# Smaller rings for two inputs, a larger ring for outputs, and new places for the moved work in a fused attention and highway kernel

## The chip, the cores and the metric

The kernel runs on one core of one Trainium2 chip. A core has five engines with instruction streams of their own: PE (matrix products), DVE and ACT (elementwise work on 128 partitions), POOL (elementwise work, and here the issue of all loads that convert from float32 to float16) and SP (here the issue of nearly all output stores). Sixteen DMA engines move the data. Within one engine's stream the order is fixed when the program is built; engines wait for one another through semaphores.

The metric is the device time of one execution in microseconds (us). Before the change the median of eight runs is 275.14 us (274.88 to 275.33).

## What is computed

Four batches (B = 4) of N = 6336 rows and C = 256 channels. The first half is a cross-covariance attention, whose attention matrix is channels by channels; the second half is a highway layer on its output:

```
qn = q / (norm of q over the N rows + 1e-6);  kn = k / (norm of k over the N rows + 1e-6)
a  = softmax over the last axis of (kn^T qn / tau)      # 256 x 256 for each batch
x  = v a                                                # N x 256 for each batch
H  = relu(x w_h);   T = sigmoid(x w_t + b_t)
out = T H + (1 - T) x
```

Inputs and output are float32. So each batch needs all rows of q and k before its 256 x 256 matrix is known, and only then can its rows of v be turned into output.

## The kernel before, in words

**Two kinds of work, run side by side.** A batch's 6336 rows are 49 tiles of 128 rows and a remainder of 64. *Pass 1* of a batch adds up, over its 49 tiles and the remainder, S = k^T q and the diagonal blocks of k^T k and q^T q (the Gram matrix G) in PSUM: `p1_tile` (L209 on), six matmuls a tile (lines L227, L230, L233). Its tiles come from loads of q and k in groups of mostly eight tiles, `load_q` and `load_k` (L127 to L137). Groups are counted through all batches here: 0 to 6 are batch 0's, 7 to 13 batch 1's, 14 to 20 batch 2's, 21 to 27 batch 3's. For some runs of tiles (`SQ_RUNS`) the q^T q part is not made on PE: ACT squares q (L275), DVE adds up the squares (L300) and PE sums the partitions (L322).

*The slots* make the output. There are 100 slots, 25 a batch; slot t handles a pair of row tiles. In slot t PE transposes the pair of v tiles (L574; DVE copies them back to SBUF as `vts`, L587), then multiplies the transposed pair by three 256 x 256 matrices of the batch (line L601): into `zbank` for the gate, into `h` for the relu branch and into `x`. ACT makes the gate `tt` by a sigmoid of `zbank` (L655) and writes the bias into the bank for the next use, the seed (L659). DVE makes `th` = max(h, 0) tt (L671) and `ux` = (tt - 1) x (L676); POOL subtracts them into an output tile (L686). The `th` and `ux` tags have four buffers each, and `h` and `x` share three PSUM banks.

*The chain* of a batch (`chain`, L308) stands between its pass 1 and its slots: norms from G, reciprocals (`invs`, L375), two diagonal tiles `dcat` on ACT (L377), the broadcast `cq` on PE (L396), the scaled logits (L409), exponentials on ACT (L419), the softmax scaling (L440), transposes of the matrix (L456), and its products with the two weight matrices (`ah`, L466), copied into the three matrices of the slots.

**The order.** Batch 0's pass 1 and chain come first, alone. Then the loop over slots (L882) interleaves: slots of batch b, the tiles of pass 1 of batch b + 1, and the steps of chain b + 1, which are placed by tables that give for each step a slot after the end of pass 1 and a position in it (`EARLY` for batch 1, `MID` for batch 2, `LAST` for batch 3). Pass 1 of batches 1 to 3 ends near slots 18, 42 and 63 (`P1_END`). From slot 64 on only the slots of batches 2 and 3 and the last chain are left.

Some steps can run ahead of their slot. `GATES` gives the number of gates in a slot where it isn't one, `TURNS` the number of pairs transposed; a 2 moves one step ahead, a 0 lets the lead shrink by one. In the slots of `PE_BIAS` the gate's bias is added by two matmuls on PE (L595) instead of by ACT's seed. `TGROUPS` names two groups of six v tiles of batch 3 that the DMA transposes instead of PE, and the slot in which SP issues it.

**Loads.** POOL issues each load in its own stream, among its subtractions. A load waits there for its buffer (`QRING` buffers each for q and k, four for v) and for the load issued eight earlier, since eight semaphores take turns. For batches 1 to 3 a planner at build time decides after which slot a load stands: it keeps a list ordered by due slot (`want`, which uses `RAMP`), holds a load back until its buffer's last reader has been emitted and until, by its own count of transfer time (`START_US`, `SLACK`), few enough are under way (`next_loads`, L737). By the same count it decides how many tiles of pass 1 go into a slot. Batch 0's groups up to `QRING` are issued at the start, ahead of the identity matrix that POOL also makes; the rest after the first tile of group 1.

**Stores.** The output tile of four slots is stored as 1 MB by SP (`send_store`, L635). Stores are held back so that loads go first: `DEFER` groups stay unsent, and each slot in `DRAIN` lowers that number by one for the rest of the run. The ring of output tiles has `ORING` buffers.

The lines that the change sets, and the functions around them:

Of the kernel before, what the change touches and what calls it, by code (L numbers as in the profile page):

```python
# [19 lines left out]
def kernel(  # L20
# [30 lines left out]
    def spans(*sizes):  # L51
        got, s0 = [], 0
        for ns in sizes:
            got.append((s0, ns))
            s0 += ns
        assert s0 == NS
        return got
# [3 lines left out]
    QALL = [(b, g) for b in range(B) for g in range(len(QG[b]))]  # L61
    QFIRST = [QALL.index((b, 0)) for b in range(B)]
    QTILES = 8
    QRING = 6
    ORING = 6
    DEFER = 5
    DRAIN = [57, 78, 74, 84]
    VG = [spans(6, 10, 12, 12, 9)] + [spans(12, 12, 12, 13)] * (B - 1)
    VTILES = 13
    VALL = [(b, g) for b in range(B) for g in range(len(VG[b]))]  # L70
# [1 line left out]
    VRING = 4  # L72
    NPAIR = (NS + 1) // 2
    LOOK = 3
    RAMP = 13
    REM_SLOT = 2
    START_US = 2

    WARM = (14, 9)

# [1 line left out]
    HEAD = sum(CHAIN0)  # L82
    P1_END = [18, 42, 63]

    GATES = {17: 2, 20: 0, 27: 2, 51: 2, 52: 2, 55: 2, 58: 0, 66: 0, 69: 0, 73: 0, 95: 2}
    TURNS = {49: 2, 51: 2, 52: 2, 53: 0, 59: 1, 60: 2, 64: 0, 72: 0, 73: 0, 93: 2}
    VTS = 9
    OLAST = 2
    TTS = 6

    TGROUPS = ((26, 6, 78), (38, 6, 79))

    PE_BIAS = (18, 21, 83, 97)

    DVE_SUBS = (98, 99)

# [2 lines left out]

    SQ_RUNS = {1: (6, 14, 21, 28), 2: (17, 26, 35), 3: (9, 23, 33)}
    SQ_TILES = 8
    SQ_CUTS = 4
    SQ_RATE = 2
    LULL = [2, 3, 0, 5]

    EARLY = {"sums": (0, "pre"), "norms": (0, "pre"), "invs": (1, "pre"), "cq": (1, "pe"), "logits": (2, "pre"), "exps": (2, "post"), "softmax": (4, "pre"), "at": (4, "pe"), "at_copy": (5, "pre"), "ahat": (5, "pe"), "ahat_copy": (6, "pre")}
    MID = {"sums": (0, "pre"), "norms": (0, "pre"), "invs": (2, "pre"), "cq": (2, "pe"), "logits": (2, "post"), "exps": (3, "post"), "softmax": (3, "post"), "at": (5, "pe"), "at_copy": (6, "pre"), "ahat": (6, "pe"), "ahat_copy": (7, "pre")}
    LAST = {"sums": (0, "pre"), "norms": (0, "pre"), "invs": (2, "pre"), "cq": (2, "pe"), "logits": (2, "post"), "exps": (3, "pre"), "softmax": (7, "pre"), "at": (8, "pe"), "at_copy": (9, "pre"), "ahat": (9, "pe"), "ahat_copy": (10, "pre")}  # L110
    PLACES = [None, EARLY, MID, LAST]

    ctx.enter_context(tc.manual_schedule())
# [7 lines left out]
    def rows(src2d):  # L121
        return src2d[0:NF, :].rearrange("(p s) c -> p s c", s=NS)
# [4 lines left out]
    def load_q(n):  # L127
        b, g = QALL[n]
        s0, ns = QG[b][g]
        q_t[n] = stream_pool.tile([P, QTILES, C], f16, tag="q_in", bufs=QRING, name=f"q{n}")  # L130
        nc.gpsimd.dma_start(out=q_t[n][:, 0:ns, :], in_=rows(q[b])[:, s0 : s0 + ns, :])  # L131

    def load_k(n):
        b, g = QALL[n]
        s0, ns = QG[b][g]
        k_t[n] = stream_pool.tile([P, QTILES, C], f16, tag="k_in", bufs=QRING, name=f"k{n}")
        nc.gpsimd.dma_start(out=k_t[n][:, 0:ns, :], in_=rows(k[b])[:, s0 : s0 + ns, :])  # L137
# [19 lines left out]
    for n, src in enumerate((q, k)):  # L157
        nc.sync.dma_start(out=rem0_32[0:REM, n, :], in_=src[0, NF:N, :])
    for n in range(QRING):
        load_q(n)  # L160
# [82 lines left out]
    def squared(b, j):  # L243

        for n, j0 in enumerate(SQ_RUNS.get(b, ())):
            count = SQ_TILES - (n > 0)
# [10 lines left out]
    def squares(b, j):  # L257
# [24 lines left out]
        add_up(len(cuts))  # L282
        more = n < len(SQ_RUNS[b]) - 1
        if more:
# [12 lines left out]
    def add_up(k):  # L297
        while k > 0 and cuts:
            dst, source = cuts.pop(0)
            nc.vector.tensor_reduce(  # L300
                out=dst, in_=source, op=AluOp.add, axis=mybir.AxisListType.XY
            )
            k -= 1
# [234 lines left out]
    def dma_transposes(t):  # L538

        for n, (s0, ns, at) in enumerate(TGROUPS):  # L540
            if at != t:
# [4 lines left out]
            vt = stream_pool.tile(  # L546
                [P, QTILES, C], f16, tag="qk"[n % 2] + "_in", bufs=QRING, name=f"vtd{n}"
            )
# [9 lines left out]

    for s0, ns, _ in TGROUPS:
        for i in range(s0 // 2, (s0 + ns) // 2):  # L560
# [29 lines left out]
    def mains(t, dst, part, seeded):  # L590
        b, i = divmod(t, NPAIR)
        mr = mr_t[b]
        if t in PE_BIAS and seeded:
            for u in range(2):
# [15 lines left out]
    def out_tile(t):  # L610
# [3 lines left out]
        if i % OG == 0:  # L614
            o_t[b] = stream_pool.tile([P, 2 * OG, C], f32, tag="o", bufs=ORING, name=f"o{t}")
        return o_t[b], 2 * (i % OG)
# [40 lines left out]
    def seed(s, z):  # L657
        if s + 2 < NSLOT and s + 2 not in PE_BIAS:
            nc.scalar.copy(out=z, in_=btb)  # L659
# [34 lines left out]
    def nominal_slot(n):  # L694

        if n < HEAD:
            return -1
        lo, base = RAMP, HEAD
        for i, e in enumerate(P1_END):
            if n < (i + 1) * (NS + 1):  # L700
                return lo + (n - base) * (e - lo) // ((i + 1) * (NS + 1) - base)
            lo, base = e + len(LULL) - 1, (i + 1) * (NS + 1)

    want = []
    for n in range(QFIRST[1] + 1, len(QALL)):
        b, g = QALL[n]
        at = nominal_slot((b - 1) * (NS + 1) + QG[b][g][0])
        for fn, key in ((load_q, "q"), (load_k, "k")):
            want.append((at, len(want), fn, n, ("q", n - QRING), QG[b][g][1]))
    for m in range(2, len(VALL)):  # L710
        b, g = VALL[m]
        at = b * NPAIR + VG[b][g][0] // 2 - LOOK - 1
# [7 lines left out]

    LANES = 8
    TILE_US = 0.305
    SLACK = 4.0
    landing = [0.0] * LANES
    landed = {}
    dma_at = [0.0]
# [10 lines left out]
    def next_loads(k, now):  # L737
        while k and want and landing[-LANES] <= now + SLACK:
            for i, (_, _, fn, arg, dep, tiles) in enumerate(want[:5]):
                held = fn is load_v and V_HELD.get(arg, -9) > slot[0]  # L740
                if not held and (dep is None or dep in ready):
                    break
            else:
                return
            want.pop(i)
            fn(arg)
            note_load((fn, arg), tiles, now)
            k -= 1
# [55 lines left out]
    for j in range(NS):  # L804
        p1_tile(0, j)
        if j == QG[0][1][0]:
            for n in range(QRING, QFIRST[1]):
                load_q(n)
# [17 lines left out]

    now = START_US
    done1 = 0
# [45 lines left out]
    def run(t, when):  # L874
        for fn in hooks.pop((t, when), []):
            fn()
# [5 lines left out]
    for t in range(NSLOT):  # L882
# [3 lines left out]
        run(t, "pre")  # L886
        zs = range(zdone, min(NSLOT, zdone + GATES.get(t, 1)))
        zdone = zs.stop
        turned = range(tdone, min(NSLOT, tdone + TURNS.get(t, 1)))
        tdone = turned.stop  # L890
# [60 lines left out]
        if t not in (end1 - 1, end1):  # L951
            next_loads(2, now)
        room = DEFER - sum(t >= at for at in DRAIN)
        out_now = 0
# [42 lines left out]
```

## Time and profile before

| what | value |
|---|---|
| median of eight runs | 275.14 us |
| the profiled execution's own time | 275.02 us |
| its span, first to last instruction | 273.2 us |
| PE busy | 252.1 us (92%), first matmul at 9.6 us, waiting for a k load |
| DVE, POOL, ACT busy | 202.8, 171.9, 164.6 us |
| DMA | 66.44 MB moved, mean 243 GB/s |
| loads (software queue) / stores (hardware queue) | 72.3% / 25.8% of the 16 DMA engines' span |
| POOL subtraction of a pair | 1.28 us (95 of them) |
| th and ux on DVE, a pair | 0.69 and 0.68 us |
| four matmuls of L601 | 0.44 us from first start to the next group's start |

Busy time of PE counts each matmul from its start to its end, and matmuls overlap: a matmul of 256 columns takes 273 ns by its record, while the next one starts 0.11 us later. So a PE that is busy all the time is one whose stream never waited, and the time that a matmul costs is the distance between starts. A wait is listed as waiter, releaser, total, number of times and longest. A load has two times: when POOL issues it and when its data has landed.

### The profile page before, as it was taken

The page shows a single profiled execution, that of the slowest core. Times are in us where ns is not written, and L with a number is a line of the kernel's source. Part 1 is how long each engine was busy: PE and PEld are TensorE (multiplying, and loading weights), DVE is VectorE, ACT ScalarE, POOL GpSimd, SP SyncE. Part 2 cuts the span into 40 slices and gives each one's busy share as a digit, 9 for nine tenths or more (in the row PEclk, how much of TensorE's full clock was granted, in tenths as well). Part 3 has the DMA queues.
Part 4 walks back from the last instruction along what each step waited for, and adds up shares of the span by engine and source line. Part 5 has one row for each costly group of instructions (what it writes and reads, how often), then busy time and mean ns, then how long its engine had stood idle before and what let it go on. Part 6 is the DMA issues. An engine that isn't in the chain of part 4 may idle for free.

```text
span 273.2 us, 6827 instructions
## 1 busy us (share of the span) xinstructions
PE 252.1 (92%) x2735; PEld 223.4 (82%) x2735; DVE 202.8 (74%) x438; ACT 164.6 (60%) x291; POOL 171.9 (63%) x191
## 2 busy tenths in 40 slices
PE   0579898999999999999999999999999999999990
PEld 0559786999999988799999888899998787999870
DVE  0060036996896876578999867689998999999983
ACT  1031046777772485488684589586745886768850
POOL 6231350899546785618879574709745897888970
PEclk9999999999999999999999999999999999999996
DMA  6999999999999999999999999999999749999466
GB/s 118 213 214 212 210 211 212 209 214 214 214 211 213 214 217 211 227 314 250 285 290 238 303 253 217 220 303 271 267 304 339 148 148 258 389 308 410 181 272 222
DMA packets 19862, 66.44 MB, mean 243 GB/s; under 512 B 4979, under 2 KB 7286, under 8 KB 16886
## 3 DMA queue, kind: packets, MB, share of 16 engines
q0 software_dynamic: 11744, 39.13, 72.3%
q1 hardware_dynamic: 8006, 26.81, 25.8%
q8 instruction: 21, 0.34, 0.5%
q10 hardware_dynamic: 80, 0.07, 0.1%
q14 instruction: 11, 0.09, 0.1%
HBM read 78.38 MB, written 25.95 MB: 382 GB/s over the span
## 4 chain that ended last, share of the span: by engine, by line
PE 80%; DMA 10%; DVE 5%; ACT 1%; issue 1%; POOL 0%; DVEq 0%; ACTq 0%; POOLq 0%
PE zbank L601 15%; PE x L601 15%; PE h L601 15%; PE S L227 14%; DMA k<-in_k_dram 10%; PE vt_bank L574 7%; PE G L230 7%; PE G L233 4%; DVE th L671 2%; DVE ux L676 1%; PE ah L466 1%; PE sums L322 1%; ACT ssb L419 0%; ACT tt L655 0%; DVE vts L587 0%
## 5 line engine op out<-in xcount | busy, mean ns | idle before, releaser
L686 POOL TENSOR_TENSOR o<-th,ux 128x512 f32<-128x512 f32 x95 | 120.7, 1280 | 38.3 <-DVE ux L676 16.3
L601 PEld LDWEIGHTS <-vts 128*128 128x128 f16 x1128 | 103.6, 98 | 13.9 <-issue 4.0
L655 ACT ACTIVATE tt<-zbank 128x512 f32<-128x512 f32 x100 | 59.1, 596 | 54.1 <-PE zbank L601 50.5
L227 PE MATMUL S<-q,k 128*128 128x256 f16 x392 | 81.9, 275 | 10.5 <-DMA k<-in_k_dram 10.5
L671 DVE SCALAR_TENSOR_TENSOR th<-h,tt 128x512 f32<-128x512 f32 (+1 forms) x104 | 69.1, 667 | 6.2 <-PE h L601 1.1
L230 PE MATMUL G<-k 128*128 128x128 f16 x392 | 73.6, 221 | 0.0
L676 DVE SCALAR_TENSOR_TENSOR ux<-tt,x 128x512 f32<-128x512 f32 (+1 forms) x104 | 68.1, 657 | 0.0
L601 PE MATMUL h<-mr,vts 128*128 128x256 f16 (+1 forms) x376 | 56.9, 273 | 0.0
L601 PE MATMUL x<-mr,vts 128*128 128x256 f16 (+1 forms) x376 | 56.9, 273 | 0.0
L659 ACT COPY zbank<-btb 128x512 f32<-128x512 f32 x94 | 55.2, 591 | 2.7
L601 PE MATMUL zbank<-mr,vts 128*128 128x256 f16 (+1 forms) x376 | 56.2, 273 | 0.1
L587 DVE COPY vts<-vt_bank 128x512 f16<-128x512 f16 x90 | 37.8, 420 | 23.5 <-PE vt_bank L574 23.3
L227 PEld LDWEIGHTS <-k 128*128 128x128 f16 x392 | 38.7, 99 | 14.6 <-DMA k<-in_k_dram 10.6
L230 PEld LDWEIGHTS <-k 128*128 128x128 f16 x392 | 38.7, 99 | 0.7
L574 PE MATMUL vt_bank<-ident,v 128*128 128x128 f16 x368 | 35.8, 219 | 0.2 <-DVE vts L587 0.2
L233 PE MATMUL G<-q 128*128 128x128 f16 x246 | 34.3, 221 | 0.0
L574 PEld LDWEIGHTS <-v 128*128 128x128 f16 x368 | 27.9, 98 | 3.5 <-issue 1.4
L131 POOL DMA_DIRECT2D q<-in_q_dram x28 | 15.9, 568 | 19.1 <-DMA q<-in_q_dram 6.5
L137 POOL DMA_DIRECT2D k<-in_k_dram x28 | 15.2, 542 | 16.2 <-DMA k<-in_k_dram 9.1
L275 ACT ACTIVATE sq<-q 128x512 f32<-128x512 f16 (+1 forms) x41 | 23.7, 617 | 0.1
L233 PEld LDWEIGHTS <-q 128*128 128x128 f16 x246 | 19.2, 99 | 1.6
L300 DVE TENSOR_REDUCE sq<-sq 128x64 f32<-128x512 f32 x28 | 18.0, 679 | 0.0
(104 smaller groups left out, 137.8 us busy)
## 6 DMA issues: line engine op xcount, KB each, us to landing
out_dram<-o SPq DMA_DIRECT2D x23, 1024.0 KB, 9.8
q<-in_q_dram POOLq DMA_DIRECT2D x20, 512.0 KB, 17.2
k<-in_k_dram POOLq DMA_DIRECT2D x20, 512.0 KB, 18.0
v<-in_v_dram POOLq DMA_DIRECT2D x11, 768.0 KB, 19.0
v<-in_v_dram POOLq DMA_DIRECT2D x3, 832.0 KB, 26.2
out_dram<-o SPq DMA_DIRECT2D x4, 256.0 KB, 3.2
q<-in_q_dram POOLq DMA_DIRECT2D x3, 320.0 KB, 18.0
k<-in_k_dram POOLq DMA_DIRECT2D x3, 320.0 KB, 17.5
```

The source lines that it names most:

```text
L227: nc.tensor.matmul(S[:, c, :], kc, qq[0:nr, :], start=first and c == 0, stop=last and c == 1)
L230: nc.tensor.matmul(G[:, c, :], kc, kc, start=first and c == 0, stop=False)
L233: nc.tensor.matmul(G[:, 2 + c, :], qc, qc, start=False, stop=last and c == 1)
L275: nc.scalar.activation(out=sq[:, o // 2, :, u : u + src.shape[1]].rearrange("p c u -> p u c"), in_=src, func=Act.Square,)
L574: nc.tensor.transpose(ps[:, u, c, 0 : nr[u]], vt[0 : nr[u], bass.ts(c, P)], ident[0 : nr[u], 0 : nr[u]],)
L587: nc.vector.tensor_copy(out=sb, in_=ps)
L601: nc.tensor.matmul(dst[0:r, u, :], vT_t[t][:, u, kt, 0:r], mr[:, part, kt, :], start=(not seeded and kt == 0 and (u == 0 or i == NPAIR - 1 ...
L655: nc.scalar.activation(out=tt_t[s], in_=z, func=Act.Sigmoid)
L659: nc.scalar.copy(out=z, in_=btb)
L671: nc.vector.scalar_tensor_tensor(out=th[pr, us, :], in0=h[pr, us, :], scalar=0.0, in1=tt[pr, us, :], op0=AluOp.max, op1=AluOp.mult,)
L676: nc.vector.scalar_tensor_tensor(out=ux[pr, us, :], in0=tt[pr, us, :], scalar=1.0, in1=x[pr, us, :], op0=AluOp.subtract, op1=AluOp.mult,)
L686: last = eng.tensor_tensor(out=ot[pr, o0 + us.start : o0 + us.stop, :], in0=th[pr, us, :], in1=ux[pr, us, :], op=AluOp.subtract,)
```

## The change

Only constants change. The rings of q and k go from six buffers to four, the ring of outputs from six to eight; six groups of stores are held back instead of five, let go in six steps instead of four; the due slots of loads, the planner's allowance (`SLACK`, `START_US`), the extra gates and transposes, the bias slots, the runs of squared tiles, the slot of the first DMA transposition and two of the chain tables are set anew. `MID` stays. The computation and the number of matmuls are the same.

```
-    QRING = 6
-    ORING = 6
-    DEFER = 5
-    DRAIN = [57, 78, 74, 84]
+    QRING = 4
+    ORING = 8
+    DEFER = 6
+    DRAIN = [59, 67, 64, 92, 72, 82]
...
-    RAMP = 13
+    RAMP = 15
...
-    START_US = 2
+    START_US = 1
...
-    GATES = {17: 2, 20: 0, 27: 2, 51: 2, 52: 2, 55: 2, 58: 0, 66: 0, 69: 0, 73: 0, 95: 2}
-    TURNS = {49: 2, 51: 2, 52: 2, 53: 0, 59: 1, 60: 2, 64: 0, 72: 0, 73: 0, 93: 2}
+    GATES = {14: 2, 19: 2, 20: 0, 22: 0, 25: 2, 27: 2, 33: 0, 54: 2, 55: 1, 60: 2, 66: 0, 68: 0, 70: 0, 95: 2}
+    TURNS = {46: 2, 47: 2, 55: 2, 65: 0, 67: 0, 79: 0, 93: 2}
...
-    TGROUPS = ((26, 6, 78), (38, 6, 79))
+    TGROUPS = ((26, 6, 73), (38, 6, 79))
...
-    PE_BIAS = (18, 21, 83, 97)
+    PE_BIAS = (8, 67, 75, 97)
...
-    SQ_RUNS = {1: (6, 14, 21, 28), 2: (17, 26, 35), 3: (9, 23, 33)}
+    SQ_RUNS = {1: (5, 20, 30), 2: (8, 18, 26, 35), 3: (10, 21, 34)}
...
     EARLY = ...
-    "softmax": (4, "pre"), "at": (4, "pe"), "at_copy": (5, "pre"), "ahat": (5, "pe"), "ahat_copy": (6, "pre")
+    "softmax": (5, "pre"), "at": (5, "pe"), "at_copy": (6, "pre"), "ahat": (6, "pe"), "ahat_copy": (7, "pre")
...
     LAST = ...
-    "invs": (2, "pre")
+    "invs": (1, "pre")
...
-    SLACK = 4.0
+    SLACK = 3
```

What this does to the streams, read from the two programs: on POOL the group loads from 12 on stand some slots later (q12 and k12 after the subtraction of slot 11 instead of after those of slots 4 and 6), while the v load that is due for the end of batch 0 moves ahead of them. The number of pass 1 tiles in each slot is the same except that slot 22 has none instead of five, and the slots after it up to 27 have three instead of two. The first store is sent in slot 25 instead of 24.

More of the change, by code (lines that the diff above doesn't have):

```diff
@@ L106 @@
     LULL = [2, 3, 0, 5]
-    EARLY = {"sums": (0, "pre"), "norms": (0, "pre"), "invs": (1, "pre"), "cq": (1, "pe"), "logits": (2, "pre"), "exps": (2, "post"), "softmax": (4, "pre"), "at": (4, "pe"), "at_copy": (5, "pre"), "ahat": (5, "pe"), "ahat_copy": (6, "pre")}
+    EARLY = {"sums": (0, "pre"), "norms": (0, "pre"), "invs": (1, "pre"), "cq": (1, "pe"), "logits": (2, "pre"), "exps": (2, "post"), "softmax": (5, "pre"), "at": (5, "pe"), "at_copy": (6, "pre"), "ahat": (6, "pe"), "ahat_copy": (7, "pre")}
     MID = {"sums": (0, "pre"), "norms": (0, "pre"), "invs": (2, "pre"), "cq": (2, "pe"), "logits": (2, "post"), "exps": (3, "post"), "softmax": (3, "post"), "at": (5, "pe"), "at_copy": (6, "pre"), "ahat": (6, "pe"), "ahat_copy": (7, "pre")}
-    LAST = {"sums": (0, "pre"), "norms": (0, "pre"), "invs": (2, "pre"), "cq": (2, "pe"), "logits": (2, "post"), "exps": (3, "pre"), "softmax": (7, "pre"), "at": (8, "pe"), "at_copy": (9, "pre"), "ahat": (9, "pe"), "ahat_copy": (10, "pre")}
+    LAST = {"sums": (0, "pre"), "norms": (0, "pre"), "invs": (1, "pre"), "cq": (2, "pe"), "logits": (2, "post"), "exps": (3, "pre"), "softmax": (7, "pre"), "at": (8, "pe"), "at_copy": (9, "pre"), "ahat": (9, "pe"), "ahat_copy": (10, "pre")}
     PLACES = [None, EARLY, MID, LAST]
```

## The prediction, made before the result was known

> **What bounds the kernel now.** I read the page first: span, busy shares and the two strips of tenths.
>
> ```profile
> span 273.2 us, 6827 instructions
> PE 252.1 (92%) x2735; PEld 223.4 (82%) x2735; DVE 202.8 (74%) x438; ACT 164.6 (60%) x291; POOL 171.9 (63%) x191
> PE   0579898999999999999999999999999999999990
> DVE  0060036996896876578999867689998999999983
> DMA  6999999999999999999999999999999749999466
> PE 80%; DMA 10%; DVE 5%; ACT 1%; issue 1%; POOL 0%; DVEq 0%; ACTq 0%; POOLq 0%
> ```
>
> PE is full from about 44 us to 262 us; the last line, the chain that ended last by engine, is PE for four fifths, and its DMA tenth is the first landing. DMA is full too, but only until about 211 us. Then I read busy time by stretch (columns: stretch, length, PE, weight loads, DVE, ACT, POOL, clock, DMA share, GB/s).
>
> ```profile
> 62.80:94.00 31.20, 31.20 (x365) 28.76 (x364) 24.20 (x51) 18.76 (x34) 20.17 (x26) 1.00 1.07 213
> 160.00:211.00 51.00, 50.99 (x569) 45.55 (x567) 41.77 (x89) 36.01 (x65) 28.59 (x29) 1.00 1.04 271
> 211.00:230.00 19.00, 18.38 (x175) 14.83 (x173) 18.57 (x40) 15.39 (x29) 16.60 (x15) 1.00 0.68 168
> 230.00:262.00 32.00, 32.00 (x323) 28.86 (x322) 30.98 (x59) 24.77 (x42) 26.44 (x23) 1.00 0.85 299
> ```
>
> Until 211 PE alone sets the pace, provided that the loads come in time. From 211 PE and DVE are both full: PE idles 0.62 us and DVE 0.43 us in the third row, 0.00 and 1.02 us in the fourth. Since the change neither adds nor removes a matmul in total, what can be won is PE's stalls. The answer on PE's waits between 44 and 270 us lists three (waiter, releaser, total us, times, longest):
>
> ```profile
> PE ah L466 <- DVE th L671: 0.4, 1, 0.4
> PE cq L396 <- ACT dcat L377: 0.3, 1, 0.3
> PE vt_bank L574 <- DVE vts L587: 0.2, 1, 0.2
> ```
>
> **The change, part by part.** The sum is against the profiled execution, 275.02 us (span 273.2 and 1.8 around it); the median shown is 275.14, 0.12 above it.
>
> *Head, 0 to 38 us: 0.* Eight loads instead of twelve stand ahead of the identity on POOL, so the identity is made near 6 us instead of 15.5, and PE's wait of 1.78 us for the remainder rows (at 16.99) goes. But batch 0's first pass ends with its data: the sixth k group lands at 33.42 (issue 14.70 plus 18.72) and nine tiles follow, at 0.44 us a tile, 37.4; the last group's products start at 37.2. k tiles are late next. The later groups now wait for a buffer too: the fifth q for group 0's products (about 14.7 instead of 7.33), the sixth for group 1's (about 19.6 instead of 12.30), the seventh for group 2's (about 23.2 instead of 17.42). Landings are 2.45 us apart, and loads already queued run until 24.8, 29.8 and 33.4 then, so no gap opens. The loads behind them on POOL (v, weights) had waited for landings at 21.8 and later and keep their times.
>
> PE will instead idle about 1.7 and 1.4 us after groups 2 and 3, until the next k lands at 24.80 and 29.75. The row: after the 1.78 us wait the S matmul still takes 0.28 us, against 0.42 at the cold start. The Trainium skill, "TensorE: Matmul & The Clock Gate", Part 1, says that the clock halves after an idle window of about 3.4 us. By the row and by the rule alike these waits cost no clock; were they to, a restart would cost what 9.6 to 12.7 us shows, about 1.5 us, and not on the path while data is late.
>
> *Ring of four, 62 to 100 us: 0, between 0 and +6.5.* This is the risk. Slots 11 to 16 eat six tiles each. Today the 8-tile groups of q and k land 2.3 to 4.8 us before use. For group 12 (the fifth full group of batch 1's pass):
>
> ```profile
> 56.40 0.57 POOL L137 DMA_DIRECT2D k<-in_k_dram  x1
> 61.27 0.57 POOL L137 DMA_DIRECT2D k<-in_k_dram  x1
> 64.33 0.57 POOL L143 DMA_DIRECT2D v<-in_v_dram  x1
> k<-in_k_dram POOLq DMA_DIRECT2D x1, 512.0 KB, 16.8
> 81.38 0.27 PE L227 MATMUL S<-q,k 128*128 128x256 f16 x1
> ```
>
> k11 issues at 56.40 and k12 at 61.27, both land 16.8 us later (73.2 and 78.1), and PE needs k12 at 81.38. After the change q12 needs group 8's buffer, whose last product starts at 67.05, and stands on POOL behind the subtract of slot 11: q12 and k12 issue near 69.8 and 70.4, about 10 us later, and a v load (9 tiles) goes ahead of them. What counts is the queue, not the 16.8: the load issued at 49.91 with 8.5 us of work ahead landed in 10.96, that is 8.5 (k8, issued at 41.33, landed after 17.08 at 58.41) plus its own 2.46. At 69.8 the queue holds work to 73.2, then v for 2.75 (9 tiles at 0.305) to 3.6 us (the spacing that its landing shows): 76.0 to 76.8. So q12 lands at 78.4 to 79.3 and k12 at 80.9 to 81.7. PE comes there later than 81.38: the second gate of slot 14 (four matmuls, 0.44) and the bias rows of slot 8 (0.22) now precede it, and seven fewer squared tiles in batch 1 add up to 0.77: 82.0 or more. Margin 0.3 to 1.1 us. The upper end, k12 keeping a dwell of 16.8 after 70.4, would be 87.2, and with the 17.5 of k13 (66.70 to 84.18) 87.9: PE 6.5 us late. I take 0, since the queue row is of the same kind and stretch. Groups 13 to 15 land near 84.7, 87.8 and 100 by the same count, against uses at 86.4, 93.5 and 103 (slot 22 lost its five tiles). Group 16 is issued near 95.8 (end of slot 19), 4.2 us before the queue runs dry at 100; a transfer's start costs 3.2 (the v load issued at 213.15 lands in 6.87, of which 12 tiles are 3.66), so the queue just stays full. Later groups are issued 17 us or more ahead of use; the nearest is group 23, issued near 150.5, landing near 163, used at 167.5.
>
> *Outputs: 0, between −0.5 and +0.5.* Stores start one slot later (25), and by slot 64 the same twelve groups are out. POOL's waits for the ring of outputs (12.3 us in three, longest 7.3) go, because a store now has nine slots instead of two before its buffer returns. Who gains is POOL; behind it, products have four th and ux buffers, and DVE shows only 0.1 us waiting for POOL. The drained stores fall in 59 to 75, while DMA has the 0.68 of the third row. The first DMA transpose moves from slot 78 to 73 on SP, ahead of one store; its v group lands near 220 to 222 and slot 73 begins near 225. The load issued at 213.15 lands in 6.87 us. Against this part stands "DMA: Bandwidth & Descriptors", Queues, rings and completion order: each DMA engine takes turns between queues, so stores can take half from these loads. By that rule the 3.7 us of transfer in those 6.87 would double and the load land near 224, by the row near 221; either is ahead of its first reader, so the sum is the same.
>
> *Bias rows: −0.2.* PE_BIAS replaces an ACT copy by two matmuls (0.111 us each) at four gates. Before, two of the four lie in the stretch where PE sets the pace (18, 21), after only one (8; 67 is issued in slot 64): 0.22 less there; the other falls in the shared stretch. Squares move seven tiles between batches 1 and 2 on PE: 0 in sum. Gates and transposes run equally far ahead (three each) at slot 63.
>
> *Last chain, slots 63 to 75: −0.4, between 0 and −1.1.* The reciprocals go from slot 65 to 64. Today ACT waits 0.72 us for them and PE starts cq 0.5 us late:
>
> ```profile
> 212.65 0.60 PE L601 MATMUL x<-mr,vts 128*128 128x256 f16 x4
> 213.57 0.70 PE L396 MATMUL cq<-dcat,taus 128*128 128x256 f32 x2 [0.32 <-ACT dcat L377]
> 213.27 0.69 DVE L671 SCALAR_TENSOR_TENSOR th<-h,tt 128x512 f32<-128x512 f32 x1 [0.17 <-PE x L601]
> ```
>
> Moved, dcat is ready near 212.4. POOL's norms end at 210.75, before DVE reaches the reciprocal near 211.2, so it does not stall DVE. PE saves 0.48 here, and at most 0.33 (218.2) and 0.30 (223.1, a seed copy behind the softmax scaling, now in a slot without a gate) more: 1.1. DVE, also full, saves only its 0.17 and what its other 0.26 of idle in this stretch gives. I take 0.4, nearer DVE's end. Two more transposes in slots 72 and 73 put 0.7 us on DVE there, paid back in 65, 67 and 79.
>
> *Chain of batch 1, one slot later: 0.* The 0.54 us hole between its ah products (107.4) stays: th still holds the PSUM bank. *Tail from 262: 0*, its placements are untouched.
>
> Sum: −0.2 −0.4 = −0.6; 275.02 becomes 274.4, or 274.5 on the median's footing.
>
> **The rivals.** *Loads late (ends slower).* One mechanism: with four buffers k12 lands after PE wants it. For: the smallest margin above, and DMA has no spare rate there (1.07). Against: queue work covers ten microseconds of later issue. It decides once k12 lands after 82.0; a landing 2 us late gives −0.6+2 = +1.4, 276.5; the far end +5.9, 280.9.
> *It changes nothing.* DVE work after 211 is the same, so what PE gains there it waits for DVE: only some 0.1 is left, 275.0.
> *PE's stalls go in full.* 0.22+1.1 = 1.3, and with DVE's 1.02 of idle after 230 in part 1.6: 273.6. For: the gap rows; against: DVE at 18.57 of 19.
>
> **How the numbers follow.** A difference under 0.2% (0.55 us) can hardly be told from none here. Forecast 0.42 (own range 274.0 to 274.9; two thirds of it under 274.6), nothing 0.14, all stalls 0.12, loads late 0.32 (nearly all over 275.7). Faster 0.28+0.12+0.01 = 0.41; same 0.14+0.12+0.02 = 0.28; slower 0.31. The range, 273.6 to 276.7, leaves out 0.05 below and 0.14 above (the late loads beyond 2 us).
>
> **What would show it.** Right: PE's wait at 15 us gone and the first pass ending at 37.4; no PE wait on DMA after 44 us; q12 issued near 70 us; cq without a wait; POOL without waits on output stores; slot 63 ending 0.2 us sooner. Wrong: a PE wait for k between 80 and 100 us, a DMA share under 1 before 200, or DVE idle for gates in slots 67 to 73.

## The result, and the profile after

The kernel after takes 274.15 us (median of 12 runs, 273.87 to 274.55) beside 275.19 us for the kernel before on the same chip (32 runs, 274.65 to 275.50): the ratio is 0.9965, with a 95% interval of 0.9957 to 0.9972. So it is faster by 0.35%, 1.0 us. The profiled execution after took 274.06 us, with a span of 272.3 us.

The page of the kernel after, the lines that answer to those of before:

```profile
span 272.3 us, 6836 instructions
PE 253.3 (93%) x2735; PEld 224.4 (82%) x2735; DVE 203.7 (75%) x438; ACT 164.7 (60%) x296; POOL 171.7 (63%) x191
PE   0699898999999999999999999999999999999990
DMA  6999999999999999999999999999999799998583
PE 82%; DMA 7%; DVE 5%; issue 2%; ACT 1%; POOL 0%; DVEq 0%; ACTq 0%; POOLq 0%
```

The number of matmuls is the same, 2735, and nothing else at this level says where 1.0 us went. The busy time by stretch is nearer (columns: stretch, length, PE, weight loads, DVE, ACT, POOL, clock, DMA share, GB/s). First before, a row that the prediction did not show; then after:

```profile
94.00:128.00 34.00, 33.62 (x371) 29.55 (x369) 24.23 (x49) 23.85 (x42) 21.82 (x25) 1.00 1.05 243
```

```profile
62.80:94.00 31.20, 31.20 (x371) 28.82 (x369) 21.80 (x47) 17.50 (x33) 16.95 (x20) 1.00 1.06 213
94.00:128.00 34.00, 34.00 (x372) 30.04 (x370) 27.22 (x54) 27.42 (x53) 25.34 (x30) 1.00 1.03 222
211.00:230.00 19.00, 18.60 (x178) 15.02 (x176) 18.50 (x39) 15.00 (x28) 16.34 (x16) 1.00 0.94 274
```

Between 94 and 128 us PE idled 0.38 us before and doesn't after. From 211 to 230 us it idles 0.40 us instead of 0.62. The list of PE's waits between 44 and 270 us (waiter, releaser, total us, times, longest) has shrunk from three lines to one:

```profile
PE vt_bank L574 <- DVE vts L587: 0.3, 1, 0.3
```

**How the traces are compared.** Apart from the head, PE's stream repeats from one execution to the next almost to 0.01 us. So the start of the last `x` matmul of each slot is a good clock: its shift against the kernel before shows in which slot time is won or lost. The head does not repeat. Slot 0 of the 14 kernels profiled here starts its last `x` matmul between 46.93 and 47.40 us, whatever was edited: 46.93 to 47.35 with four buffers, 47.04 to 47.40 with six. The kernel after stands 0.16 us ahead there, which is within that spread and is put down to no edit. Below, "net shift" is the shift of a slot less the shift of slot 0; a minus is a gain. "At the end" it is taken at the last instruction of the execution. The shift moves by a whole step where one kernel has a gate or transposition earlier than the other, so it is only read where both are equally far ahead, as at slot 63 and at the end.

| kernel | edit | ratio to before, 95% interval | net shift at slot 63 | at the end |
|---|---|---|---|---|
| after | all | 0.9965 (0.9957 to 0.9972) | −0.76 | −0.78 |
| bias alone | before with the new bias slots | 1.0003 (0.9995 to 1.0012) | −0.23 | −0.01 |
| chain alone | before with the later chain of batch 1 | 0.9988 (0.9979 to 0.9997) | −0.54 | −0.54 |
| reciprocals alone | before with `invs` in slot 64 | 1.0004 (0.9995 to 1.0013) | −0.01 | −0.01 |
| buffers alone | before with the new rings and held stores | 1.0039 (1.0026 to 1.0052) | +1.01 | +1.01 |
| buffers and chain | before with both | 0.9973 (0.9962 to 0.9983) | −0.54 | −0.55 |
| places alone | before with the new gates and transposes | 0.9994 (0.9985 to 1.0003) | −0.37 | −0.11 |
| places, reciprocals | before with both | 0.9988 (0.9979 to 0.9997) | −0.36 | −0.29 |

The kernel after, with one part put back or changed (net shift against after):

| kernel | edit | ratio to before, 95% interval | net shift at slot 63 | at the end |
|---|---|---|---|---|
| old chain | chain of batch 1 as before | 1.0020 (1.0011 to 1.0030) | +1.36 | +1.34 |
| old reciprocals | `invs` in slot 65 | 0.9983 (0.9974 to 0.9992) | −0.01 | +0.38 |
| old buffers | rings and held stores as before | 0.9984 (0.9976 to 0.9993) | +0.07 | +0.37 |
| DVE loaded | subtractions of slots 45 and 80 on DVE | 0.9989 (0.9980 to 0.9998) | +0.01 | +0.57 |
| no bias on PE | no bias slots | 0.9935 (0.9922 to 0.9948) | −0.22 | −0.77 |

### The profile page after: what moved, and what is told of

Read it like the earlier page. It is cut to its first block, busy times and chain, and to the rows that moved or that the text cites. A ratio compares the mean times of both kernels' runs of the same rounds, so it can differ in the third digit from the quotient of the medians.

```text
span 272.3 us, 6836 instructions
## 1 busy us (share of the span) xinstructions
PE 253.3 (93%) x2735; PEld 224.4 (82%) x2735; DVE 203.7 (75%) x438; ACT 164.7 (60%) x296; POOL 171.7 (63%) x191
## 4 chain that ended last, share of the span: by engine, by line
PE 82%; DMA 7%; DVE 5%; issue 2%; ACT 1%; POOL 0%; DVEq 0%; ACTq 0%; POOLq 0%
PE zbank L601 15%; PE S L227 15%; PE h L601 15%; PE x L601 15%; DMA k<-in_k_dram 7%; PE vt_bank L574 7%; PE G L230 7%; PE G L233 4%; DVE th L671 2%; PE ah L466 1%; DVE ux L676 1%; DVE vts L587 1%; DVE at_sb L332 1%; ACT tt L655 0%; POOL q L131 0%
## 5 line engine op out<-in xcount | busy, mean ns | idle before, releaser
L227 PE MATMUL S<-q,k 128*128 128x256 f16 x392 | 82.5, 278 | 10.7 <-DMA k<-in_k_dram 10.6
L275 ACT ACTIVATE sq<-q 128x512 f32<-128x512 f16 (+1 forms) x46 | 24.3, 570 | 0.0
L332 DVE SCALAR_TENSOR_TENSOR at_sb<-G,ident 128x128 f16<-128x128 f32 x16 | 3.7, 288 | 25.5 <-PE G L233 25.4
## 6 DMA issues: line engine op xcount, KB each, us to landing
k<-in_k_dram POOLq DMA_DIRECT2D x3, 320.0 KB, 10.6
```

Source lines behind the costliest of these rows:

```text
L227: nc.tensor.matmul(S[:, c, :], kc, qq[0:nr, :], start=first and c == 0, stop=last and c == 1)
L275: nc.scalar.activation(out=sq[:, o // 2, :, u : u + src.shape[1]].rearrange("p c u -> p u c"), in_=src, func=Act.Square,)
```

## The experiments

### Bias slots alone

```
-    PE_BIAS = (18, 21, 83, 97)
+    PE_BIAS = (8, 67, 75, 97)
```

> The kernel before with only the new set of gates whose bias comes from matmuls (8, 67, 75, 97 for 18, 21, 83, 97). The prediction's theory: two matmuls of 0.111 us are saved in the stretch where PE alone sets the pace, so 0.22 us faster than before (about 275.0 against 275.2). Rival, that ACT, which has to copy the bias at two more gates there, or DVE behind it, takes it back: 0.0. The trace should show the last matmul of slot 62 some 0.2 us earlier.

Measured: no change, 1.0003. At slot 63 the net shift is −0.23 us, as forecast. But then it comes back: the bias rows of gate 67, issued in slot 64, cost 0.22 us there, those of 75 cost 0.22, and those of 83, which are gone, give 0.22. The net shift at the end is −0.01. So a gate's bias on PE costs its two matmuls wherever it stands, also where DVE is full. A choice of four other slots moves nothing; whether having fewer of them does is asked by the last run.

### The chain of batch 1 alone

```
-    "softmax": (4, "pre"), "at": (4, "pe"), "at_copy": (5, "pre"), "ahat": (5, "pe"), "ahat_copy": (6, "pre")
+    "softmax": (5, "pre"), "at": (5, "pe"), "at_copy": (6, "pre"), "ahat": (6, "pe"), "ahat_copy": (7, "pre")
```

> The kernel before with only the chain of batch 1 one slot later, so that its ah products stand in slot 24 (the pair with 64 rows) instead of slot 23. The prediction says 0.0: th still holds the PSUM bank and the wait of 0.54 us stays. The theory from the trace after says that the wait goes, because th24 is done before the second ah product: 0.5 us faster (274.6 to 274.7). A third possibility: the wait goes and the gate behind it takes a part, 0.2 to 0.3 us.

Measured: faster, 0.9988, −0.3 us with an interval of −0.6 to −0.1; by the slots −0.54 us, all of it in slots 23 and 24. Here is the hole in the kernel before (timeline: start, us, engine, line, operation, idle time before it and its releaser), and then the same products in this run:

```profile
107.04 0.60 PE L466 MATMUL ah<-wht,at_sb 128*128 128x256 f16 x4
...
107.28 0.69 DVE L671 SCALAR_TENSOR_TENSOR th<-h,tt 128x512 f32<-128x512 f32 x1 [0.48 <-PE x L601]
...
108.03 0.60 PE L466 MATMUL ah<-wht,at_sb 128*128 128x256 f16 x4 [0.38 <-DVE th L671]
```

```profile
109.33 0.75 DVE L671 SCALAR_TENSOR_TENSOR th<-h,tt 128x256 f32<-128x256 f32 x2 [0.23 <-PE h L601]
109.79 1.05 PE L466 MATMUL ah<-wht,at_sb 128*128 128x256 f16 x8
```

`h`, `x` and the two `ah` products of batch 1 share the three PSUM banks, so the second product takes the bank of that slot's `h` and must wait until `th` has read it. In slot 23 `th` ends at 107.97, and the second product starts at 108.03 instead of 107.48 (the first's start plus four times 0.11). In slot 24 the pair has a tile of 64 rows. Its `x` takes longer, `th` is done at 110.08, and the second product, due at 109.79 + 0.44 = 110.23, finds its bank free. All eight matmuls run as one group. The longer `x` phase (0.22 us) is not the whole of it. In slot 23 `th` also starts late, which makes 0.37 of the 0.54 us (see "What stays open"); with `th` in time a hole of 0.17 us is left there, as the run with the new places shows below.

### The reciprocals of the last chain alone

```
     LAST
-    "invs": (2, "pre")
+    "invs": (1, "pre")
```

> The kernel before with only the reciprocals of the last chain in slot 64 instead of 65. The prediction says 0.4 us faster (PE's wait of 0.48 us for dcat goes and PE keeps most of it). The theory from the trace after: that wait goes, but DVE is full from 211 to 262 us, so PE waits about as long for DVE one to five slots later, and the time is the same as before within 0.1 us.

Measured: no change, 1.0004. PE's wait for `dcat` is gone, and the net shift in slot 66 is −0.59. In slot 67 it is −0.11 and in slot 69 −0.01, because PE now waits for DVE at the next two transpositions:

```profile
215.56 0.38 PE L574 MATMUL vt_bank<-ident,v 128*128 128x128 f16 x4 [0.33 <-DVE vts L587]
218.61 0.27 PE L574 MATMUL vt_bank<-ident,v 128*128 128x128 f16 x2 [0.27 <-DVE vts L587]
```

In the kernel before, on its own, this part is worth nothing.

### The buffers and held stores alone

```
-    QRING = 6
-    ORING = 6
-    DEFER = 5
-    DRAIN = [57, 78, 74, 84]
+    QRING = 4
+    ORING = 8
+    DEFER = 6
+    DRAIN = [59, 67, 64, 92, 72, 82]
```

> The kernel before with only the buffers: four each for q and k, eight for outputs, six groups of stores held back in the new slots. The prediction: 0.0 within 0.5 us either way, no PE wait for a load after 44 us. The rival, loads late: PE waits for k12 or a later group, 1.4 us or more slower. If the earlier first landing of the kernel after (9.36 against 9.56 us) comes from fewer loads ahead, it shows here, 0.2 us faster; if it varies by run, it doesn't.

Measured: slower, 1.0039 (+1.0 us). No load is late for PE. The cost appears in one place, in a wait that the kernel before doesn't have. PE's waits between 44 and 270 us in this run, and the timeline around the first of them:

```profile
PE at L456 <- ACT mr L440: 0.6, 1, 0.6
PE ah L466 <- DVE th L671: 0.4, 1, 0.4
PE cq L396 <- ACT dcat L377: 0.3, 1, 0.3
PE vt_bank L574 <- DVE vts L587: 0.2, 1, 0.2
```

```profile
99.99 0.60 PE L601 MATMUL x<-mr,vts 128*128 128x256 f16 x4
...
100.42 0.60 PE L601 MATMUL zbank<-mr,vts 128*128 128x256 f16 x4
...
101.92 0.16 DVE L436 RECIPROCAL rinv<-rs 128x2 f32<-128x2 f32 x1
...
102.11 0.91 ACT L440 ACTIVATE mr<-ssb,rinv 128x256 f16<-128x256 f32 x2 [0.86 <-DVE rinv L436]
...
102.67 0.68 PE L456 MATMUL at<-ident,mr 128*128 128x128 f16 x4 [0.55 <-ACT mr L440]
```

Between the `x` matmuls of slot 21 (99.99) and `zbank` of slot 22 (100.42) nothing is left. In the kernel before five tiles of q and k stand there, from 100.66 to 102.87, 2.2 us of PE's work. With four buffers their group is issued later, the program puts the five tiles into slots 23 to 27, one more in each, and slot 22 lasts 1.53 us instead of 3.75. The softmax (`rinv`, then `mr` on ACT) has a fixed place in slot 22, and its transposes `at` stand at the slot's end. PE gets there 0.99 us too early: the gaps between matmul starts exceed their usual ones by 0.72 before `at` and 0.27 within it. That is nearly all of the 1.01 us of the table. The rings of q and k and the settings of the stores were not run apart, but no store is sent before slot 24, so that only the rings of q and k can have moved these tiles.

### Buffers and chain together

The two edits above, in the kernel before.

> The kernel before with two parts: the buffers and held stores, and the chain of batch 1 one slot later. Alone they gave 1.0 us slower and 0.5 us faster (by the slots' ends). If they simply add, 0.5 us slower than before. Theory: in the later slot the softmax has the products of slots 23 and 24 as cover, so both waits go (0.99 us for the softmax, 0.54 us between the ah products): 0.5 us faster than before, and then the four buffers cost nothing.

Measured: faster, 0.9973; by the slots −0.55 us. The parts don't add: the buffers cost 1.01 us with the chain in its old place and nothing with the chain a slot later. The softmax then stands in slot 23, and three tiles between slots 22 and 23 cover it. The transposes wait for nothing:

```profile
103.46 0.16 DVE L436 RECIPROCAL rinv<-rs 128x2 f32<-128x2 f32 x1
103.65 0.91 ACT L440 ACTIVATE mr<-ssb,rinv 128x256 f16<-128x256 f32 x2 [1.24 <-DVE rinv L436]
104.83 0.39 PE L456 MATMUL at<-ident,mr 128*128 128x128 f16 x4
```

`mr` is ready near 104.56, and PE arrives at 104.83. These two parts give 0.55 of the 0.78 us of the whole change.

### The chain put back in the kernel after

> The kernel after with only the chain of batch 1 put back one slot earlier (softmax in slot 22 and the ah products in slot 23, as before). If the chain's place is worth only the wait between the ah products, 0.5 us slower than after (274.6 to 274.7 where after has 274.15). The theory from the run with the buffers alone: slot 22 has lost its q and k tiles to the later loads, so the at transposes of that slot also wait for the softmax on ACT, 0.99 us there; then 1.3 to 1.6 us slower than after, 275.5 to 275.7. If the prediction was right that the chain's place is worth nothing, the time of after.

Measured: 1.0020, slower than the kernel before and 0.55% slower than after. By the slots it is 1.36 us, all of it in slots 22 to 25. Of this 1.18 us are at the transposes and 0.17 us between the `ah` products:

```profile
103.08 0.90 ACT L440 ACTIVATE mr<-ssb,rinv 128x256 f16<-128x256 f32 x2
...
103.64 0.68 PE L456 MATMUL at<-ident,mr 128*128 128x128 f16 x4 [0.74 <-ACT mr L440]
```

So the place of this chain alone decides whether the whole change is a gain or a loss.

### The reciprocals put back in the kernel after

> The kernel after with only the reciprocals of the last chain put back from slot 64 to 65. The prediction's step: 0.4 us slower than after (274.5). The theory from the run of this part alone, which changed nothing: 0.0 to 0.1 us slower; PE waits for dcat again, and no longer for DVE in the next slots.

Measured: 0.9983, and 0.38 us more by the slots, where the same edit on the kernel before gave 0.01. The theory of DVE's being full did not carry over. PE waits for `dcat` again, but what it loses there (+0.80 in slot 66) comes back only in part (to +0.40 in slot 68 and after):

```profile
213.15 0.70 PE L396 MATMUL cq<-dcat,taus 128*128 128x256 f32 x2 [0.54 <-ACT dcat L377]
```

### New places without and with the reciprocals

The slots of extra gates and transposes (`GATES`, `TURNS`) of the kernel after, in the kernel before; then the same with `invs` in slot 64.

> The kernel before with only the new slots of gates and transposes. Counted from the last matmul of slot 63 to the end, this should be the same as before within 0.2 us if these places matter only together with the reciprocals. If they free PE's last stretch by themselves, 0.4 us less there.

> The kernel before with the new slots of gates and transposes and the reciprocals of the last chain in slot 64. Theory: slots 65 and 67 have no transposes now, so DVE has room just there, and what PE saves at cq is kept: from the last matmul of slot 63 to the end 0.4 us less than with the places alone. Rival: 0.40 us in the kernel after came from something else (loads, outputs, bias); then 0.0, as with the reciprocals alone.

Measured: 0.9994 and 0.9988. From slot 63 to the end the places alone cost 0.26 us and the places with the reciprocals 0.07 us. So with the new places the reciprocals are worth 0.19 us there, against 0.00 in the kernel before and 0.38 in the kernel after. It is an interaction, and its direction is as expected, but half the size remains unexplained by the places. In the second run PE still waits in slot 66 where the kernel after waits 0.18 us less:

```profile
215.59 0.60 PE L601 MATMUL x<-mr,vts 128*128 128x256 f16 x4 [0.32 <-DVE th L671]
```

The run with the old buffers, next, has the same wait, so the rest goes with the buffers and held stores. Up to slot 63 both runs gain 0.37 us, which was not expected: the hole between the `ah` products shrinks from 0.54 to 0.17 us, because `th` of slot 23 starts in time there.

### The old buffers in the kernel after

> The kernel after with the buffers and held stores of before (six each for q and k, six for outputs, five groups held back in four steps). If four buffers cost nothing once the chain of batch 1 is a slot later, the time of after within 0.2 us. If the later loads still cost something, up to 0.5 us faster. If the new places of gates and transposes are right only for the new loads, slower, by up to 1 us.

Measured: 0.9984, and 0.37 us more by the slots: 0.07 up to slot 63, 0.24 in slots 64 to 67, 0.08 later. So in the new setting the new buffers and held stores, taken together, are a small gain. POOL shows why they can be: with six output buffers it waits 5.2 us for a store between 200 and 270 us, with eight not at all.

```profile
POOL o L686 <- DVE ux L676: 6.2, 18, 0.9
POOL o L686 <- DMA out_dram<-o: 5.2, 1, 5.2
```

How this reaches DVE, for which PE waits in slot 66 of this run (0.32 us before an `x`, as with the old rings and new places), was not isolated.

### More work for DVE

```
-    DVE_SUBS = (98, 99)
+    DVE_SUBS = (45, 80, 98, 99)
```

> The kernel after with the output's subtraction of slots 45 and 80 on DVE (0.69 us each) instead of POOL (1.3 us each). Theory: in slot 45 PE alone sets the pace, and DVE has room, so nothing moves there; in slot 80 DVE is as full as PE, so part of 0.69 us shows, 0.3 to 0.7 us slower in all, and the last matmuls of slots 46 to 79 stand where after has them. Rival, that DVE isn't a bound after 211 us: no difference anywhere. If POOL is what holds the last stretch, faster.

Measured: 0.9989, and +0.57 us by the slots. None of it falls at slot 45: the net shift from slot 46 to 80 stays within 0.01 us. In slot 80 the added 0.69 us on DVE pushes a transposition back, and the shift is 0.44 after slot 82 and 0.57 from slot 85 on:

```profile
238.63 0.69 DVE L686 TENSOR_TENSOR o<-th,ux 128x512 f32<-128x512 f32 x1
239.71 0.38 PE L574 MATMUL vt_bank<-ident,v 128*128 128x128 f16 x4 [0.27 <-DVE vts L587]
```

So DVE has room at slot 45, and at slot 80 it is a bound: there 0.57 of the added 0.69 us is lost. Each was tried in one slot.

### No bias on PE

```
-    PE_BIAS = (8, 67, 75, 97)
+    PE_BIAS = ()
```

> The kernel after with no gate whose bias comes from matmuls: ACT copies the bias for all, four more copies of 0.59 us. The slots' ends with other gates chosen showed each such gate at 0.22 us of PE wherever it stood (slots 8, 17, 20, 64, 75, 83). Theory: up to 0.9 us faster than after, 273.3, if ACT is in time everywhere. Rival: in slots 64 to 97, where two gates can fall in one slot, PE waits for ACT's copy, 0.6 us or more at each of the three places; then no change or up to 1 us slower.

Measured: 273.28 us (273.03 to 273.62), 0.9935 of the kernel before: by the ratios 1.8 us faster than before and 0.8 us faster than after. The net shift falls by 0.22 us in slot 8, in slot 64 and in slot 75, and by 0.1 near slot 96, where PE waits 0.14 us for the bias copy. ACT's four further copies of 0.59 us are otherwise hidden: between 211 and 262 us it is busy 41.57 of 51 us, and PE's one listed wait there is the old one.

```profile
211.00:262.00 51.00, 50.59 (x494) 43.51 (x491) 49.85 (x98) 41.57 (x72) 43.31 (x37) 1.00 0.92 299
```

## Why the prediction was right, and where its steps were not

The forecast was 274.5 us, 0.6 below the kernel before, and the time is 274.15, 1.0 below. Faster was the right side (given a chance of 0.41), and the range holds it. But that the sum came out near is in part luck. It was to come as 0.2 us up to slot 63 and 0.4 us behind it; it came as 0.76 and 0.02. One term was 0.54 us too small, another 0.22 too large.

**Head: 0.** Right. The pass of batch 0 ended at 37.3 us (forecast 37.4), the wait at 15 us is gone, and k was late after groups 2 and 3 by 0.25 and 1.37 us (forecast 1.7 and 1.4). That neither wait costs clock is right of this execution: after the longer one the first S matmul takes 0.28 us, and the others stay at 0.27. It is not safe as a rule, since in another run the clock fell after such a wait (last section). The wait after group 2 is so short because the first, slow matmuls lasted longer in this execution: in the five kernels with four buffers where they lasted 2.8 to 3.6 us it is 1.2 to 1.6 us.

```profile
29.61 0.28 PE L227 MATMUL S<-q,k 128*128 128x256 f16 x1 [1.21 <-DMA k<-in_k_dram]
...
29.78 0.27 PE L227 MATMUL S<-q,k 128*128 128x256 f16 x1
```

The start of slot 0 moved by 0.16 us, inside the spread of the head.

**Ring of four: 0, with k12 as the risk.** The count of the queue was right:

```profile
68.94 0.57 POOL L131 DMA_DIRECT2D q<-in_q_dram  x1
69.51 0.54 POOL L137 DMA_DIRECT2D k<-in_k_dram  x1
```

```profile
82.77 0.27 PE L227 MATMUL S<-q,k 128*128 128x256 f16 x1
```

k12 was issued at 69.51 (forecast 70.4), landed at 81.06 (80.9 to 81.7) and was first used at 82.77 (82.0 or more). The slack of 1.7 us was even larger than the 0.3 to 1.1 forecast, and the rival of late loads fell. But the ring costs something all the same, by a way that no rival named: later loads took five tiles out of slot 22, and these tiles were the cover of the softmax. The prediction saw that "slot 22 lost its five tiles" and used it only as time won for a load. Without the later chain this costs 1.01 us in the kernel before, and the whole change is then slower than before (1.0020): the forecast would have been on the wrong side. One sign that the prediction had named for being wrong did show, a DMA share under 1 before 200 us. Group 16 was issued at 97.0 us (forecast 95.8), and the queue ran short for a moment; yet PE waited for no load. The rows from 98 to 103 us, before and then after:

```profile
98.00:103.00 5.00, 5.00 (x59) 4.47 (x57) 3.49 (x8) 4.08 (x9) 3.66 (x5) 1.00 1.05 216
```

```profile
98.00:103.00 5.00, 5.00 (x58) 4.47 (x57) 4.35 (x11) 4.88 (x9) 4.48 (x7) 1.00 0.97 171
```

**Outputs: 0.** POOL's waits for stores are gone, as forecast. Together with the rings of q and k they are worth 0.37 us in the kernel after, inside the 0.5 us allowed. The first DMA transposition waits for a v load that landed at 222.81, after 10.6 us instead of 6.9 before; the answers on transfers, for stretches around the issue, before, then after, then in the kernel after with the old buffers and held stores:

```profile
v<-in_v_dram POOLq DMA_DIRECT2D x1, 768.0 KB, 6.9
```

```profile
v<-in_v_dram POOLq DMA_DIRECT2D x1, 768.0 KB, 10.6
```

```profile
v<-in_v_dram POOLq DMA_DIRECT2D x1, 768.0 KB, 7.0
```

By the row alone it should have landed near 221, or, from its issue at 212.23, at 219.1. The Trainium skill, "DMA: Bandwidth & Descriptors", Queues, rings and completion order, says that an engine goes round the queues that have work, a packet at a time; by that rule the prediction worked out 224, and adding its 3.7 us to the 219.1 gives an estimate of 222.8, which is what was measured. The DMA share of 211 to 230 us is 0.94 where it was 0.68, which agrees with stores taking from loads. So do the other runs: this load takes 6.7 to 7.2 us in all seven kernels with the old buffers and held stores, in which no 1 MB store is issued while it is under way, and 10.3 to 10.8 us in all seven with the new ones, in which three are. The load was still ahead of its reader at 225.31.

**Bias rows: −0.2.** Wrong: 0. The gain of 0.22 by slot 63 is there, but the step took the rows that moved into the shared stretch for free. They cost the full 0.22 each.

**Last chain: −0.4.** In the kernel after, the reciprocals are worth 0.38 us, what was forecast. The reason given, that PE keeps most of its wait, holds only there: on the kernel before they give nothing. And the stretch as a whole from slot 63 to the end gained 0.02 us, since the bias rows of two gates came in at 0.22 each and one left, and the places alone cost 0.26. The rival "it changes nothing", with DVE the cause, was right of this part in the kernel before and wrong of it in the kernel after.

**Chain of batch 1: 0.** Wrong: −0.54, most of the gain, and the failing step was the sentence "th still holds the PSUM bank". It does in slot 23. The chain moves to slot 24, where the pair is another: its `x` phase is longer, `th` does not start late, and it ends before the bank is needed. The bank rule was right, the slot was not looked at.

Taken from the runs, up to slot 63: buffers and chain −0.54, bias −0.23, in sum −0.77 where −0.76 was measured (the 0.37 that the places gain there is part of the same hole). From slot 63 on: bias +0.22, places with the reciprocals +0.07, buffers and held stores −0.30 (the run with the old ones, 0.37 less 0.07), in sum −0.01 where −0.02 was measured. The runs of squared tiles, the planner's constants and the slot of the DMA transposition were not run alone. The sum leaves nothing for them, though effects that cancel would not show. The profiled executions differ by 0.94 us in span, the 0.78 and the head's 0.16, which varies; the medians differ by 1.0 us, with an interval of 0.8 to 1.2.

**What stays open.** `th` of slot 23 starts late in the kernel before: its inputs and the DVE operation ahead of it are done at 106.80, it starts at 107.28. Most `th` follow within 0.11 us. The same gap of 0.48 us is there with the buffers alone, where POOL's subtraction ended at 106.22 and DVE was free at 105.80, and one of 0.47 to 0.49 us with the bias and with the reciprocals alone. It is not there with the new places or in the kernel after. It makes 0.37 of the 0.54 us hole, and the work of POOL and ACT does not explain it. What the four cases share is that `th` starts 0.06 to 0.07 us after the `x` matmuls of its slot end (107.21 in the kernel before), although it reads `h` and `tt` and not `x`. With the new places alone it starts at 106.58, 0.3 us before they end. Whether it waited for them in the four is not shown.

## What to carry to other kernels

When loads get later, ask not only whether they land in time but which work leaves its slot with them: tiles that are never late can still be the cover of a dependent chain, and a chain with a fixed place then waits (1.0 us here, and nothing once the chain stood one slot later). Edits of such a schedule do not add: the same edit was worth 0.54 us on six buffers, 1.56 on four (+1.01 to −0.55) and 1.36 in the final kernel, so a price taken from one setting holds for that setting. PE is full throughout here, and its bias matmuls cost their start-to-start time in nearly every place, also where DVE is full too; leaving them out (eight matmuls, 0.8 us) gained more than placing them did.

## What the runs showed of the hardware

TensorE's first matmuls run at 0.39 to 0.42 us for S, and the change to 0.27 us came 5.8 us after the first one in the kernel after, 5.0 us in the kernel after with the old chain, and 2.8 to 4.1 us in the other twelve kernels, where the same tiles stand at the head. The granted clock in the row of 10 to 38 us is 1.00 all the same. It cost nothing here, since k comes later than PE needs it until 37 us.

```profile
9.41 0.39 PE L227 MATMUL S<-q,k 128*128 128x256 f16 x1 [9.41 <-DMA k<-in_k_dram]
...
14.82 0.40 PE L227 MATMUL S<-q,k 128*128 128x256 f16 x1
15.22 0.27 PE L227 MATMUL S<-q,k 128*128 128x256 f16 x1
```

The Trainium skill, "TensorE: Matmul & The Clock Gate", Part 1, puts the warm-up at about 3.4 us of sustained work; 5.8 us in one execution is longer than that, and the 2.8 us of another is shorter.

The clock also fell again once, in the run of the reciprocals alone, whose head is that of the kernel before. PE idles 1.91 us there, works on the remainder rows and the first seeds of the gate banks for 1.6 us, and then on S at full speed for 0.4 us. After that its matmuls are slow for 3.4 us, with a granted clock of 0.52:

```profile
16.60 0.28 PE L227 MATMUL S<-rem 64*128 64x256 f16 x1 [1.91 <-DVE rem L191]
...
18.91 0.42 PE L227 MATMUL S<-q,k 128*128 128x256 f16 x1
```

```profile
18.60:22.00 3.40, 3.40 (x29) 2.91 (x26) 1.63 (x6) 2.54 (x4) 0.82 (x2) 0.52 1.06 213
```

The kernel before has nearly the same wait (1.78 us) and stays fast. So an idle time of less than 2 us can be followed by slow matmuls, which the prediction's figure of 3.4 us would have ruled out; whether it mattered what PE did in the 1.6 us behind the wait is not shown. It cost nothing at slot 0 (47.40 us, in the spread of the others): the wait of about 1 us for k near 29 us in the kernel before is not there in this run.

The other surprise is how exactly PE's stream repeats. The 0.54 us hole came out at 0.53 to 0.54 us in the four kernels that kept it, and a shift that has settled stays within 0.02 us for 40 slots.
